# Token block steps of a spectral mixing kernel in eight rotating places, with the set loads spread anew

## The chip, the cores and the metric

The kernel runs on one core of a Trainium2 chip. The metric is the device time of one execution in microseconds (us). The core has five engines that work side by side: TensorE (PE in the profile, with PEld for its weight loads) multiplies matrices into PSUM, VectorE (DVE) does elementwise arithmetic, ScalarE (ACT) does copies and functions, GpSimd (POOL) and SyncE (SP) are used here above all to issue DMA transfers. Semaphores order them.

## The reference

The input is one sequence of S = 2048 tokens with D = 640 channels. It is normalized, goes through a Fourier mixing layer and a gated layer, and both are added to the input:

```python
a = jnp.einsum("bsd,ed->bse", x, dft_hid_re)
b = jnp.einsum("bsd,ed->bse", x, dft_hid_im)
y = jnp.einsum("ts,bse->bte", dft_seq_re, a) - jnp.einsum("ts,bse->bte", dft_seq_im, b)
...
gate = jnp.einsum("bsd,df->bsf", x, W_gate)
up = jnp.einsum("bsd,df->bsf", x, W_up)
gate = gate * (lambda x, dt: x.astype(dt))(gate > 0, gate.dtype)
h = gate * up
return jnp.einsum("bsf,fd->bsd", h, W_down)
...
x = A_x
xn = _layernorm(x, axis=-1)
return x + _A_ref(xn, A_dft_seq_re, A_dft_seq_im, A_dft_hid_re, A_dft_hid_im) + _B_ref(xn, B_W_gate, B_W_up, B_W_down)
```

The gated layer has F = 1728 columns. All data are fp32.

## The kernel before, in words

Every fp32 operand of TensorE is split into a high part (a copy rounded to the fp32r type, made by ScalarE) and a low part (the operand minus its high part, made by VectorE); `split` at L124 and L125 does both. A product of two operands is then three matmuls, high by high, high by low and low by high (`mm3`, L130 to L132). All block products are arranged as in Strassen's method, with seven products of sums and differences of blocks in place of eight.

The program has three phases.

1. **Mixing along the sequence.** The 2048 output positions are worked in four chunks c of 512. For each chunk, the Fourier matrices come from HBM in pieces of 128x1024 (`raw`, six buffers; `tk`, four) and are multiplied by the normalized tokens, which lie in `xs_early` and `xs_late`. A unit such as `T30` is one stream name (T1, T2, B22, T3, T4) and one group of tokens (0 to 3). T1 and B22 units are 18 matmuls, T2, T3 and T4 units 12. Each unit has a `load` (DMA on SP), a `prepare` (VectorE builds the difference at L613, then `split` into a ring of three `cb` buffers), a `run` (TensorE) and a `finish` (sums at L511 to L600, stored by POOL into `pq`). The normalization of the tokens is done during chunk 0, in a 32 KB region `r1` of each partition (`ln_tile`).
2. **Gate and up.** 26 units over the columns of the gate and up weights (`z`, split into `gw`), multiplied by *sets*: sums and differences of blocks of the transposed normalized tokens, kept split in SBUF (`xs_early` for the sets called A, `r1` for those called B). The 64 columns that are left (1728 - 13 x 128) have the *rest weights* (`st`, split into `wr`, L867 to L870), used first in this phase.
3. **Projection** back, with W_down and the hidden Fourier matrices, and the output.

The sets must be made in phase 1. `token_sets` does it for the first half (q = 1) in six *steps*, numbered 0 to 5. A step loads the row statistics (`mr`, L336 or L354) and a block of transposed tokens (`a` or `ab`, L337 or L355) on POOL's queue, normalizes them on VectorE (L340 and L341, or L360 and L361), makes four differences (L367), splits the results in one or two *halves*, and stores high and low part in HBM (L399 and L400 to `halves`, named `set` in the profile). Steps 0 and 1 have one half of 512 columns, steps 2 to 5 two halves of 1024. `load_halves` later brings the finished sets into SBUF (L687): K units load the four B sets, A units the five A sets. An A set lies where tokens lay in `xs_early`, so it waits for the T2 units that read them.

A list `todo` holds units and steps in program order, and `drive(4, 2)` walks through it: at entry i it first calls what was deferred to i, then the load of entry i, the prepare of entry i - 2, the finish of i - 5 and the run of i - 4. The steps of the tokens stand ten entries apart, starting after the last normalization sums of chunk 0. In phase 1 each engine's order comes from a planner that models times and takes the earliest entry that it believes ready; `tc.keep_in_program_order` fixes the first addition of a step, and `tc.issue_after(ins)` puts an instruction behind `ins` on its engine's queue. In phase 2, TensorE, VectorE and ScalarE follow the program's order, while SP and POOL are planned.

`late["dma"]` is the newest load of a Fourier matrix piece. The weights of phase 2 (`Weights`, L764) are already put behind it. `lead_load` (L962 to L965) brings the first operands of phase 3 into two `stage` buffers; `lead_split` splits them at the end of phase 2.

Before the change, a step of phase 1 works in the two buffers of the pool `stage` (both are taken by one step of two halves), and the high part of each half goes to `hi`, a pool with one buffer.

Of the kernel before, what the change touches and what calls it, by code (L numbers as in the profile page):

```python
# [7 lines left out]
F32 = mybir.dt.float32  # L8
F32R = mybir.dt.float32r
# [3 lines left out]
P = 128  # L13
# [3 lines left out]
W2 = 2 * CH  # L17
HC = CH // 2
NCHUNK = S // CH
# [8 lines left out]
NF = F // P  # L28
# [17 lines left out]
NRAW = 10 * P  # L46
# [12 lines left out]
def fnet_reglu_kernel(  # L59
# [15 lines left out]
    nc = tc.nc  # L75
    keep = ctx.enter_context(tc.tile_pool(name="keep", bufs=1))
# [11 lines left out]
    get_r1 = lambda dtype: r1_p.tile([P, len(SETS_B) * 2 * W2], dtype, name="r1")  # L88
# [6 lines left out]
    halves = dram_p.tile([NSET, P, 2, W2], F32, name="set1")  # L95

    firsts = [dram_p.tile([P, 3, CH], F32, name=f"first{c}") for c in range(NCHUNK)]
    pqd = [dram_p.tile([2, P, KD, CH], F32, name=f"pq{c}") for c in range(NCHUNK)]
# [24 lines left out]
    def split(hi, lo, src):  # L123
        nc.scalar.activation(hi, src, AF.Copy)  # L124
        return nc.vector.tensor_tensor(lo, src, hi.bitcast(F32), op=OP.subtract)  # L125
# [23 lines left out]
    def defer(units, f):  # L149

        deferred.setdefault(now[0] + units, []).append(f)
# [4 lines left out]
    ph1 = ExitStack()  # L156
# [2 lines left out]
    tk = ph1.enter_context(tc.tile_pool(name="tk", bufs=NH))  # L159
    sums = ph1.enter_context(tc.tile_pool(name="sums", bufs=1))  # L160
    small = ph1.enter_context(tc.tile_pool(name="small", bufs=2))
    high_p = ph1.enter_context(tc.tile_pool(name="high", bufs=1))
    late_p = ph1.enter_context(tc.tile_pool(name="late", bufs=1, side="right"))
    xs_late = late_p.tile([P, D * S // P], F32R, name="xs_late")

# [19 lines left out]
    late = {}  # L185
# [133 lines left out]
        pin(high(1, 1))  # L319
        late["ln"] = pin(low(1, 1))[-1].ins  # L320

    def token_sets(q, step, stage=stage, unit=None):

        ch = xt[:, q * W2 : (q + 1) * W2].rearrange("(k p) t -> k p t", p=P)
        st_r = rows[:, q * W2 : (q + 1) * W2]
        tt = nc.vector.tensor_tensor
        part = lambda st, i: st[:, i * CH : (i + 1) * CH]
        t = {}

        if step < 2:  # L330
            cs = slice(step * CH, (step + 1) * CH)

            def load():
                t["mr"], t["a"] = stage(), stage()[:, :CH]
                for i in range(2):
                    nc.gpsimd.dma_start(part(t["mr"], i), st_r[i : i + 1, cs].to_broadcast([P, CH]))  # L336
                nc.gpsimd.dma_start(t["a"], ch[4][:, cs])  # L337

            def make():
                tc.keep_in_program_order(tt(t["a"], t["a"], part(t["mr"], 0), op=OP.add))  # L340
                tt(t["a"], t["a"], part(t["mr"], 1), op=OP.mult)  # L341

            made = [([make], "a", lambda v: halves[X4][:, v, cs], lambda ap: ap)]
            keep_whole = lambda: nc.gpsimd.dma_start(sets[X4][:, cs], t["a"])
        else:
            k, hs = (step - 2) // 2, (step - 2) % 2 * HC
            hs = slice(hs, hs + HC)
            cols = lambda ap: ap.rearrange("p (c t) -> p c t", c=2)
            cs = slice(k * CH + hs.start, k * CH + hs.stop)

            def load():
                t["mr"], t["ab"] = stage(), stage()
                for i in range(2):
                    nc.gpsimd.dma_start(cols(part(t["mr"], i)), cols(st_r[i : i + 1])[:, :, hs].to_broadcast([P, 2, HC]))  # L354
                    nc.gpsimd.dma_start(cols(part(t["ab"], i)), cols(ch[k + 2 * i])[:, :, hs])  # L355

            def make():
                mr, ab = t["mr"], t["ab"]
                for i in range(2):
                    tc.keep_in_program_order(tt(part(ab, i), part(ab, i), part(mr, 0), op=OP.add))  # L360
                    tt(part(ab, i), part(ab, i), part(mr, 1), op=OP.mult)  # L361

            def more():

                mr, ab = t["mr"], t["ab"]
                (a0, a1, b0, b1), (t1, t2, t3, t4) = ([st[:, i * HC : (i + 1) * HC] for i in range(4)] for st in (ab, mr))
                sub = lambda o, i0, i1: tt(o, i0, i1, op=OP.subtract)  # L367
                sub(t1, a1, a0)
                sub(t2, b1, t1)
                sub(t3, b1, a1)  # L370
                sub(t4, b0, t2)

            by_set = lambda ap: ap.rearrange("p (i t) -> p i t", i=4)
            made = [([make, more], "ab", lambda v: halves[B11 : B11 + 4, :, v, cs].rearrange("i p t -> p i t"), by_set),
                    ([], "mr", lambda v: halves[T1 : T1 + 4, :, v, cs].rearrange("i p t -> p i t"), by_set)]

            def keep_whole():
                for i, st in ((B11, t["ab"]), (T1, t["mr"])):
                    nc.gpsimd.dma_start(sets[i : i + 4, :, cs].rearrange("i p t -> p i t"), by_set(st))

        if unit:
            unit(load, made[0][0], keep_whole)
            return

        def begin():
            load()
            for i, (make, name, place, view) in enumerate(made):

                def halve(make=make, name=name):
                    for m in make:  # L390
                        m()
                    src = t[name]
                    if "h" not in t:
                        t["h"] = high_p.tile([P, W2], F32R, name="hi")
                    split(t["h"][:, : src.shape[1]], src.bitcast(F32R), src)

                def keep(name=name, place=place, view=view):
                    src = t[name]
                    nc.gpsimd.dma_start(place(0), view(t["h"][:, : src.shape[1]].bitcast(F32)))  # L399
                    nc.gpsimd.dma_start(place(1), view(src))  # L400

                defer(6 + 2 * i, halve)
                defer(7 + 2 * i, keep)

        todo.append((begin, idle, idle, idle))

    def raw():
# [273 lines left out]
    def load_halves(i):  # L681

        def load():
            if "sets_b" not in late:
                late["sets_b"] = {1: get_r1(F32R)}
            t, b = set_place(1, i)
            nc.sync.dma_start(t[:, b : b + 2 * W2].bitcast(F32), halves[i].rearrange("p v t -> p (v t)"))  # L687

        todo.append((load, idle, idle, idle))

# [20 lines left out]
    def phase(c, names):  # L711


        for n in names.split():
            if n == "K":
                load_halves(first_sets.pop(0))
            elif n == "A":
                load_halves(early_sets.pop(0))
            elif n[0] == "W":
                sums_124(int(n[1]))  # L720
            elif n[0] == "V":
                sums_3(int(n[1]))
            elif n[0] == "B" and n[2] == "1":
                first_stream(int(n[3]), n[:3], int(n[4]))
            else:
                stream(c, n[:-1], int(n[-1]))
            if n == "V3":
                free[0] = len(todo) + 2
            if free[0] is not None and len(todo) >= free[0] and steps:
                token_sets(*steps.pop(0))  # L730
                free[0] = len(todo) + SPACE
# [6 lines left out]
    for c in range(1, NCHUNK - 1):  # L738
        phase(c, "T10 T11 T12 T13 T20 B220 T21 B221 T22 T23 B222 B223 T30 T31 T32 T33 T40 T41 T42 T43")
    assert not steps, len(steps)  # L740
    phase(NCHUNK - 1, "T10 T11 T12 T13 T20 K B220 K T21 K B221 K T22 A T23 A B222 B223 T30 A T31 A T32 A T33 T40 T41 T42 T43")
    assert not early_sets and not first_sets
    drive(4, 2)
    ph1.close()
# [9 lines left out]
    NU = 2 * NF  # L754
# [3 lines left out]
    class Weights:  # L758


        def __init__(self, n):
            self.z2 = pool("z").tile([P, 2 * P + NZ], F32, name="z")
            with tc.issue_after(late["dma"]):
                nc.sync.dma_start(self.z2[:, :NRAW], wgu[n % NF])  # L764
            self.n, self.z = n, self.z2[:, 2 * P :]

        def sums(self):
# [20 lines left out]
    weights, held = {}, {}  # L788
# [76 lines left out]

    def rest_weights():
        rest["st"] = st = stage()[:, :D]  # L867
        nc.sync.dma_start(st, wrest)
        rest["w"] = w = pool("wr").tile([P, 2, D], F32R, name="wr")
        split(w[:, 0], w[:, 1], st)  # L870

# [79 lines left out]
    def pair(k0, n):  # L951

        if k0 < KD:
            return hid[0, k0 : k0 + n], hid[1, k0 : k0 + n]
        f = 2 * (k0 - KD)
        w = wd[f * P : (f + 2 * n) * P].rearrange("(k i p) n -> k i p n", i=2, p=P)
        return w[:, 0], w[:, 1]
# [3 lines left out]

    def lead_load():  # L962
        lead["r"], lead["s"] = r, s = stage(), stage()[:, : 2 * 3 * P].rearrange("p (k n) -> p k n", k=2)
        nc.sync.dma_start(r, pqd[2][0][:, :2])
        nc.sync.dma_start(s, pair(0, 2)[0].rearrange("k p n -> p k n")[:, :, : 3 * P])  # L965

    def lead_split():
        t = get_gw[1]().rearrange("p v z -> p (v z)")
# [12 lines left out]
    def place(i):  # L981
        if i % 2 == 0:
            spare[i // 2] = pool("prep").tile([P, Y12 + 2 * P], F32, name="pw")
        return spare[i // 2][:, i % 2 * W2 : (i % 2 + 1) * W2]
# [280 lines left out]
```

## Time and profile before

| | us |
|---|---|
| median of 3 runs | 1048.72 |
| lowest and highest run | 1046.82 and 1049.37 |
| the profiled execution | 1048.9 |
| its span, first to last instruction | 1047.1 |
| TensorE busy | 1028.8 |
| VectorE busy | 802.6 |
| ScalarE busy | 432.9 |
| GpSimd busy | 103.1 |

The mean granted TensorE clock is 0.995 of full speed. A line of the profile names the source line (L613), the engine, the operation, and the tiles as out<-in. In a timeline, the first two numbers are the start and the length in us, and brackets at the end hold how long the engine was idle before the instruction and what released it. In a list of waits, the numbers are the total in us, how often, and the longest. Phase 1 ends near 418 us, phase 2 near 750 us.

### The profile page before, as it was taken

To read this page: it belongs to the slowest core of one execution; us is meant where nothing else is said; L and a number is where in the kernel's file an instruction comes from. 1 tells how busy PE (TensorE), PEld (TensorE's weight loads), DVE (VectorE), ACT (ScalarE), POOL (GpSimd) and SP (SyncE) were. 2 spreads that over 40 slices of the span, in tenths; PEclk is the share of its full clock that TensorE was granted. 3 is DMA by queue.
4 is the path that set the end of the run, shared out by engine and by line. 5 is a ranking of instruction groups with operands and counts; after the bars stand their busy time and mean duration, and the time that the engine had idled before them with its cause. 6 is when DMAs were issued, how large, how long until landed. Compare 5 with 4: busy or idle time off the path is not lost.

```text
span 1047.1 us, 12457 instructions
## 1 busy us (share of the span) xinstructions
PE 1028.8 (98%) x4528; PEld 848.1 (81%) x4528; DVE 802.6 (77%) x1072; ACT 432.9 (41%) x544; POOL 103.1 (10%) x166
## 2 busy tenths in 40 slices
PE   8999999999799999999999999999999999999998
PEld 7888888887587778888888888888888888888886
DVE  7957977977879677687787988877588666786664
ACT  5754443333333333333343544444355423552521
POOL 2000011102212000431110000010000000000000
PEclk9999999999899999999999999999999999999999
DMA  8974754957858895784355666663598736986453
GB/s 306 348 237 165 260 152 149 340 183 266 304 213 271 338 410 214 214 265 155 145 192 171 209 234 215 232 222 131 178 392 286 219 101 215 386 293 228 151 163 120
DMA packets 101469, 242.73 MB, mean 232 GB/s; under 512 B 11553, under 2 KB 50977, under 8 KB 98849
## 3 DMA queue, kind: packets, MB, share of 16 engines
q1 hardware_dynamic: 83664, 171.68, 48.4%
q0 software_dynamic: 17744, 70.26, 18.5%
q8 instruction: 35, 0.57, 0.2%
q14 instruction: 26, 0.20, 0.1%
HBM read 182.12 MB, written 58.74 MB: 230 GB/s over the span
## 4 chain that ended last, share of the span: by engine, by line
PE 85%; issue 6%; DMA 4%; DVE 3%; POOL 1%; ACT 1%; SPq 0%; ACTq 0%; DVEq 0%; POOLq 0%
PE ps L130 28%; PE ps L131 28%; PE ps L132 28%; PE ps L1162 1%; PE ps L501 1%; DMA raw<-in_dft 1%; DMA set<-st 1%; DMA set<-hi 1%; DMA tk<-in_dft 1%; DVE cb L125 1%; DMA rw<-hd 1%; ACT cb L124 1%; DVE tk L613 0%; PE ps L473 0%; DVE raw L613 0%
## 5 line engine op out<-in xcount | busy, mean ns | idle before, releaser
L132 PE MATMUL ps<-cb,wt 128*128 128x512 f32 x390 | 151.9, 390 | 0.4 <-DVE wt L125 0.4
L130 PE MATMUL ps<-cb,wt 128*128 128x512 f32 x390 | 151.8, 389 | 0.0
L131 PE MATMUL ps<-cb,wt 128*128 128x512 f32 x390 | 151.7, 389 | 0.0
L125 DVE TENSOR_TENSOR cb<-rw,cb 128x1024 fp32r<-128x1024 f32 x83 | 94.1, 1133 | 69.7 <-ACT cb L124 67.8
L124 ACT ACTIVATE cb<-rw 128x1024 fp32r<-128x1024 f32 x83 | 81.9, 987 | 149.4 <-PE ps L132 122.8
L124 ACT ACTIVATE cb<-raw 128x1024 fp32r<-128x1024 f32 x78 | 82.5, 1059 | 125.5 <-PE ps L132 108.0
L125 DVE TENSOR_TENSOR cb<-raw,cb 128x1024 fp32r<-128x1024 f32 x78 | 95.2, 1220 | 39.3 <-ACT cb L124 36.0
L131 PE MATMUL ps<-cb,xs_late 128*128 128x512 f32 x256 | 100.7, 394 | 3.8 <-DVE cb L125 3.8
L130 PE MATMUL ps<-cb,xs_late 128*128 128x512 f32 x256 | 100.2, 393 | 4.4 <-ACT cb L124 4.4
L132 PE MATMUL ps<-xs_early,gw 128*128 128x512 f32 x260 | 101.1, 389 | 0.0
L130 PE MATMUL ps<-xs_early,gw 128*128 128x512 f32 x260 | 101.1, 389 | 0.0
L131 PE MATMUL ps<-xs_early,gw 128*128 128x512 f32 x260 | 101.1, 389 | 0.0
L132 PE MATMUL ps<-cb,xs_late 128*128 128x512 f32 x256 | 100.4, 392 | 0.0
L131 PE MATMUL ps<-cb,xs_early 128*128 128x512 f32 x238 | 92.7, 390 | 1.8 <-DVE cb L125 1.8
L130 PE MATMUL ps<-cb,xs_early 128*128 128x512 f32 x238 | 93.2, 393 | 0.8 <-ACT cb L124 0.8
L132 PE MATMUL ps<-cb,xs_early 128*128 128x512 f32 x238 | 92.1, 389 | 0.0
L121 ACT ACTIVATE gw<-z 128x1024 fp32r<-128x1024 f32 (+1 forms) x52 | 57.6, 1110 | 77.8 <-DVE z L774 75.4
L132 PEld LDWEIGHTS ps<-cb,wt 128*128 128x128 f32 x390 | 73.2, 188 | 15.9 <-DVE wt L125 0.7
L131 PEld LDWEIGHTS ps<-cb,wt 128*128 128x128 f32 x390 | 73.2, 188 | 15.5 <-DVE cb L125 0.2
L130 PEld LDWEIGHTS ps<-cb,wt 128*128 128x128 f32 x390 | 73.2, 188 | 15.2
L121 ACT ACTIVATE u<-ps 128x512 f32<-128x512 f32 x52 | 31.2, 599 | 93.2 <-PE ps L132 93.2
L784 DVE TENSOR_TENSOR gw<-z,gw 128x1024 fp32r<-128x1024 f32 (+1 forms) x52 | 64.7, 1284 | 3.8 <-ACT gw L121 3.8
(192 smaller groups left out, 1937.9 us busy)
## 6 DMA issues: line engine op xcount, KB each, us to landing
raw<-in_dft SPq DMA_DIRECT2D x94, 512.0 KB, 5.7
wt<-wparts SPq DMA_DIRECT2D x66, 256.0 KB, 3.2
z<-in_wgu SPq DMA_DIRECT2D x26, 640.0 KB, 4.0
hd<-ob POOLq DMA_DIRECT2D x26, 512.0 KB, 3.7
rw<-hd SPq DMA_DIRECT2D x24, 512.0 KB, 6.4
wparts<-pw POOLq DMA_DIRECT2D x11, 1024.0 KB, 4.1
tk<-in_dft SPq DMA_DIRECT2D x16, 512.0 KB, 6.6
rw<-pq SPq DMA_DIRECT2D x16, 512.0 KB, 7.3
```

Of the source, the lines that this page charges most:

```text
L121: return nc.scalar.activation(o, i, AF.Copy)
L124: nc.scalar.activation(hi, src, AF.Copy)
L125: return nc.vector.tensor_tensor(lo, src, hi.bitcast(F32), op=OP.subtract)
L130: nc.tensor.matmul(ps, wh, mh, start=first, stop=False, skip_group_check=more)
L131: nc.tensor.matmul(ps, wh, ml, start=False, stop=False, skip_group_check=more)
L132: nc.tensor.matmul(ps, wl, mh, start=False, stop=last, skip_group_check=more)
L501: nc.tensor.matmul(E[c, key], xn_part(j, d)[v == 1], b[c][0][:, int(v == 2), j], start=j == 0 and v == 0, stop=False)
L784: tt(self.w[:, 1, cs], self.z[:, cs], self.w[:, 0, cs].bitcast(F32), op=OP.subtract)
L1162: nc.tensor.matmul(B[key], wr[:, v, es], hr[:, cs], start=False, stop=v == 1, skip_group_check=not new)
```

## The change

A step of phase 1 takes each of its buffers (statistics, block, and one high part for each half) from eight places of 4 KB in turn, in one tile over the 32 KB of `r1`, which the normalization has left by then and which the B sets take afterwards. The pool `high` goes. The two halves of a step are deferred by 6 and 7 entries (before: 6 and 8), and the stores by 8 and 9 (before: 7 and 9). In the last chunk, three of the four K entries and two A entries stand together behind T23, and the fourth K stands at the very end; before, the four K stood between T20 and T22. Every K and A load, the rest weights' load and the lead loads get an instruction behind which they must be issued: the newest matrix load for the first three kinds, the last load of phase 2's weights for the lead. Steps of phase 2 (`unit` and `place` given) work as before.

```diff
@@ -159,7 +159,6 @@
-    high_p = ph1.enter_context(tc.tile_pool(name="high", bufs=1))
@@ -319,7 +318,15 @@
-    def token_sets(q, step, stage=stage, unit=None):
+    def token_sets(q, step, place=None, unit=None):
+
+        def work():
+            if "work" not in late:
+                late["work"] = get_r1(F32)
+            i = late["places"] = (late.get("places", -1) + 1) % 8
+            return late["work"][:, i * W2 : (i + 1) * W2]
+
+        stage = place or work
@@ -390,17 +397,15 @@
                     src = t[name]
-                    if "h" not in t:
-                        t["h"] = high_p.tile([P, W2], F32R, name="hi")
-                    split(t["h"][:, : src.shape[1]], src.bitcast(F32R), src)
+                    t["h" + name] = h = work()[:, : src.shape[1]]
+                    split(h.bitcast(F32R), src.bitcast(F32R), src)
 
                 def keep(name=name, place=place, view=view):
-                    src = t[name]
-                    nc.gpsimd.dma_start(place(0), view(t["h"][:, : src.shape[1]].bitcast(F32)))
-                    nc.gpsimd.dma_start(place(1), view(src))
-
-                defer(6 + 2 * i, halve)
-                defer(7 + 2 * i, keep)
+                    for v, part in enumerate((t["h" + name], t[name])):
+                        nc.gpsimd.dma_start(place(v), view(part))
+
+                defer(6 + i, halve)
+                defer(8 + i, keep)
@@ -684,7 +689,8 @@
             t, b = set_place(1, i)
-            nc.sync.dma_start(t[:, b : b + 2 * W2].bitcast(F32), halves[i].rearrange("p v t -> p (v t)"))
+            with tc.issue_after(late["dma"]):
+                nc.sync.dma_start(t[:, b : b + 2 * W2].bitcast(F32), halves[i].rearrange("p v t -> p (v t)"))
@@ -738,7 +744,7 @@
-    phase(NCHUNK - 1, "T10 T11 T12 T13 T20 K B220 K T21 K B221 K T22 A T23 A B222 B223 T30 A T31 A T32 A T33 T40 T41 T42 T43")
+    phase(NCHUNK - 1, "T10 T11 T12 T13 T20 B220 T21 B221 T22 T23 K K K A A B222 B223 T30 A T31 A T32 A T33 T40 T41 T42 T43 K")
@@ -761,7 +767,7 @@
             with tc.issue_after(late["dma"]):
-                nc.sync.dma_start(self.z2[:, :NRAW], wgu[n % NF])
+                self.ins = nc.sync.dma_start(self.z2[:, :NRAW], wgu[n % NF]).ins
@@ -865,7 +871,8 @@
-        nc.sync.dma_start(st, wrest)
+        with tc.issue_after(late["dma"]):
+            nc.sync.dma_start(st, wrest)
@@ -961,8 +968,9 @@
-        nc.sync.dma_start(r, pqd[2][0][:, :2])
-        nc.sync.dma_start(s, pair(0, 2)[0].rearrange("k p n -> p k n")[:, :, : 3 * P])
+        with tc.issue_after(weights[NU - 1].ins):
+            nc.sync.dma_start(r, pqd[2][0][:, :2])
+            nc.sync.dma_start(s, pair(0, 2)[0].rearrange("k p n -> p k n")[:, :, : 3 * P])
```

## The prediction

> **What bounds the kernel now.** I read the page first: TensorE (PE) is busy for 1028.8 us, 98% of the span. So the question is only where it stands still or runs slowly. The waits of TensorE, listed by who is waited for, give the sizes; the busy time by stretch gives the place and the granted clock.
>
> ```profile
> span 1047.1 us, 12457 instructions
> PE ps L131 <- DVE cb L125: 5.6, 3, 2.5
> PE ps L130 <- ACT cb L124: 5.2, 2, 4.4
> 26.20:261.10 234.90, 234.90 (x1037) 194.14 (x1035) 183.01 (x240) 107.96 (x139) 23.41 (x38) 1.00 0.68 233
> 261.10:276.25 15.15, 8.26 (x36) 6.42 (x36) 13.79 (x20) 4.14 (x4) 2.30 (x3) 0.98 0.78 290
> 276.25:282.65 6.40, 6.40 (x15) 4.63 (x15) 5.17 (x5) 2.12 (x2) 2.01 (x3) 0.50 0.99 289
> 282.65:392.00 109.35, 105.47 (x463) 86.34 (x462) 86.72 (x91) 38.79 (x40) 13.94 (x20) 1.00 0.83 310
> 392.00:1042.90 650.90, 650.49 (x2866) 537.35 (x2864) 492.65 (x663) 264.20 (x329) 54.07 (x91) 1.00 0.63 214
> ```
>
> The columns are stretch, length, then busy time of PE, weight loads, DVE, ACT, POOL, then clock and DMA. From 26.2 to 261.1 us TensorE never stops, and after 392 it loses 0.41 us before the tail. All else is lost between 261 and 392 us, in five stops, which the timeline of TensorE shows:
>
> ```profile
> 263.62 0.50 PE L131 MATMUL ps<-cb,xs_late 128*128 128x512 f32 x1 [2.51 <-DVE cb L125]
> 276.25 1.22 PE L130 MATMUL ps<-cb,xs_late 128*128 128x512 f32 x2 [4.38 <-ACT cb L124]
> 338.58 0.50 PE L131 MATMUL ps<-cb,xs_late 128*128 128x512 f32 x1 [1.34 <-DVE cb L125]
> 347.83 0.50 PE L130 MATMUL ps<-cb,xs_early 128*128 128x512 f32 x1 [0.79 <-ACT cb L124]
> 368.70 0.50 PE L131 MATMUL ps<-cb,xs_early 128*128 128x512 f32 x1 [1.75 <-DVE cb L125]
> ```
>
> They add to 2.51 + 4.38 + 1.34 + 0.79 + 1.75 = 10.77 us. Behind the longest, the clock stands at 0.50 for 6.40 us, so half of that, 3.20 us, is lost too. That is 13.97 us in all, the most that the change can win if it touches nothing else.
>
> **Stops at 261 and 272 us: step 3 of the token work.** The timelines of POOL, VectorE (DVE) and ScalarE (ACT) there:
>
> ```profile
> 251.71 0.73 POOL L355 DMA_DIRECT2D st<-in_xt  x1
> 259.40 0.69 DVE L360 TENSOR_TENSOR st<-st 128x512 f32<-128x512 f32 x1 [4.27 <-DMA st<-in_xt]
> 265.72 0.77 POOL L399 DMA_DIRECT2D set<-hi  x1 [8.24 <-ACT hi L124]
> 270.39 1.06 ACT L124 ACTIVATE hi<-st 128x1024 fp32r<-128x1024 f32 x1 [4.16 <-DVE sa L511]
> 271.48 1.23 DVE L125 TENSOR_TENSOR st<-st,hi 128x1024 fp32r<-128x1024 f32 x1 [1.36 <-ACT hi L124]
> 273.83 1.22 DVE L613 TENSOR_TENSOR raw<-raw,tk 128x1024 f32<-128x1024 f32 x1
> 275.14 1.06 ACT L124 ACTIVATE cb<-raw 128x1024 fp32r<-128x1024 f32 x1 [3.69 <-DVE raw L613]
> ```
>
> VectorE stands 4.27 us at the step's first addition (L360), because POOL issued its load only at 251.71; both `stage` buffers were still in use by step 2. The low part that TensorE wants queues behind it: stop one. Then ScalarE stands at 270.39 with the second `hi<-st`. The row names `DVE sa`, but the first half's store left only at 265.72, and the row below, of the waits of all engines, shows `hi` waiting for that store: there is one `hi` buffer. VectorE loses another 1.36 us, the subtraction at 273.83 comes late, the high part at 275.14 later, and TensorE stops for 4.38 us.
>
> ```profile
> ACT hi L124 <- DMA set<-hi: 10.4, 3, 4.2
> ```
>
> **Stops at 337, 347 and 367 us: step 5, and the SP queue.**
>
> ```profile
> 333.94 1.06 ACT L124 ACTIVATE hi<-st 128x1024 fp32r<-128x1024 f32 x1 [4.05 <-DMA set<-hi]
> 335.03 1.23 DVE L125 TENSOR_TENSOR st<-st,hi 128x1024 fp32r<-128x1024 f32 x1 [0.71 <-ACT hi L124]
> 324.00:347.00 23.00, 21.66 (x95) 17.32 (x93) 22.29 (x29) 8.55 (x9) 3.41 (x5) 1.00 0.76 248
> SPq L868 <- DMA set<-st: 6.4, 1, 6.4
> 348.89 0.76 POOL L400 DMA_DIRECT2D set<-st  x1 [6.73 <-DVE tk L613]
> 356.59 0.86 SPq L687 DMA_DIRECT2D r<-set  x2
> 357.54 0.41 SPq L617 DMA_DIRECT2D raw<-in_dft  x1
> 366.28 1.23 DVE L613 TENSOR_TENSOR tk<-raw,tk 128x1024 f32<-128x1024 f32 x1 [7.43 <-DMA raw<-in_dft]
> ```
>
> In step 5 the single `hi` holds ScalarE again (4.05 us), VectorE waits 0.71 us of 23.00 and is busy for 22.29. On SP, the rest weights' load (L868) stands 6.4 us for a `stage` buffer with chunk 3's matrices behind it; then the set loads (L687) stand until 356.59 for step 5's last store (348.89), and the next `raw` goes only at 357.54. VectorE waits 7.43 us for it and TensorE 1.75.
>
> **The change part by part.** No matmul, addition, copy or transfer is added or taken away; their lengths stay.
>
> *Eight places for the steps.* A step's load no longer waits for the step before it (places of step 4 are those of step 2, twenty units back), so the 4.27 us go. Each half has its own high place, so ScalarE's waits at `hi` (10.4 us) go, and with them the 1.36 and 0.71 us on VectorE. What becomes late next is VectorE itself. A step still brings it this, from the groups by line between 320 and 347 us:
>
> ```profile
> L125 DVE TENSOR_TENSOR st<-st,hi 128x1024 fp32r<-128x1024 f32 x2 | 2.4, 1221 | 0.7 <-ACT hi L124 0.7
> L367 DVE TENSOR_TENSOR st<-st 128x256 f32<-128x256 f32 x4 | 1.5, 418 | 0.0
> L360 DVE TENSOR_TENSOR st<-st 128x512 f32<-128x512 f32 x2 | 1.4, 684 | 0.0
> L361 DVE TENSOR_TENSOR st<-st 128x512 f32<-128x512 f32 x2 | 1.4, 684 | 0.0
> ```
>
> That is 6.7 us. A T3 or T4 unit is 12 matmuls of 0.2265 us (1037 in 234.90 us, above), so 2.72 us, and wants 2.44 us of VectorE (two operations of 1.22): only 0.28 us a unit is spare. So in these two places I let VectorE bound TensorE. Near step 3, stops of 2.51 + 4.38 = 6.89 us less the idle VectorE time that goes, 4.27 + 1.36 = 5.63, leaves 1.26. Near step 5, 1.34 + 0.79 = 2.13 less 0.71 leaves 1.42. Together 2.68 us stay; between nothing (the planner fills earlier slack) and the whole 9.02 I take this, since VectorE's rows there stand without a gap. Steps 2 and 4 lie beside the longer T2 and B22 units, where TensorE had no stop.
>
> *Second half at +7 instead of +8, stores at +8 and +9.* VectorE's 1.22 us and ScalarE's 1.06 come a unit sooner, ahead of one more low part: 0 to 1.22 us for step 3, and for step 5; I take 0, as the subtraction that TensorE ends up waiting for stands behind both halves either way. POOL's two stores move back; behind them stand only the stores of sums and the next step's load, which now has a whole step to land. If that cover fails the 4.27 us return.
>
> *The set loads (K, A).* Three K go behind T23's matrix, the fourth behind T43's; each is put behind the newest matrix load on SP. The matrices of T21 to T23 pass them, so the 7.43 us wait and the 1.75 us stop go. The K still cannot go before step 5's last store. What queues behind them now is T30 to T33. T30 is 192 matmuls behind chunk 3's first (72 of T1, 48 of T2, 72 of B22), 43.5 us at 0.2265: near 391 us if T10 begins at 347.83, while the K stood until 356.59. With that cover gone a late T30 would stop TensorE one for one; I take 0, with bounds of 0 and the 1.75 us of today's stop. A wait for TensorE's reads of xs_early, as they do today.
>
> *Rest and lead.* The 6.4 us on SP end: T10's loads, now issued from 341.69, move up, worth nothing beyond the 0.79 us already counted. The rest weights now land later. The rows that bound this:
>
> ```profile
> 388.25 6.40 SPq L617 DMA_DIRECT2D raw<-in_dft  x4
> 409.49 0.80 SPq L764 DMA_DIRECT2D z<-in_wgu  x2
> 410.62 0.72 ACT L124 ACTIVATE wr<-st 128x640 fp32r<-128x640 f32 x1
> 417.56 0.39 PE L130 MATMUL ps<-xs_early,wr 128*128 128x512 f32 x1
> 701.80 0.33 SPq L764 DMA_DIRECT2D z<-in_wgu  x1
> 746.72 1.78 ACT L124 ACTIVATE gw<-st 128x1024 fp32r<-128x1024 f32 x2
> ```
>
> The last matrix goes by 394.65 and ScalarE wants `st` at 410.62: 16 us for a load and one K, today's K loads included in 1.75 us of damage at most. Cost 0; at worst, behind both z loads, it leaves at 410.3 and TensorE wants the split at 417.56, so 7 us less a landing. The lead loads go from 378 and 412 us to behind 701.80 and are wanted at 746.72: 45 us of cover, cost 0.
>
> **Sum.** The profiled execution took 1048.9 us (span 1047.1 and 1.8 around it), 0.2 above the median of the runs, 1048.72. So 1048.9 - 10.77 - 3.20 + 2.68 = 1037.6, and 1037.4 against the median.
>
> **The clock.** The 2.51 us stop was followed by matmuls at full clock up to 271.9 (0.98 over that stretch), the 4.38 us stop by 0.50. The Trainium skill, TensorE: Matmul & The Clock Gate, Part 1, says that half clock follows at least one idle window of about 3.4 us, and that this window runs freely. This trace agrees: 4.38 brought it, 2.51 did not; by it the remaining pieces keep full clock unless they join into one stop over 3.4 us.
>
> **Rivals.**
> *One long stop stays.* At the hand-over from chunk 1 to chunk 2 the T43 subtraction stays late, because step 3's halves are now bunched. Against it: the DMA wait behind it goes. Price: 4.38 + 3.20 stay instead of 1.26, 1037.4 + 6.3 = 1043.7. By the page's rule, named above, the same stop costs its clock again.
> *The loads do not come earlier.* The planner keeps a step's load behind the stores of the step before, now at +8 and +9, one unit ahead of the load. For: POOL's row at 251.71. Then 2.51 and 4.38 and the clock stay, the rest goes: 1048.7 - 3.88 + 1.42 = 1046.3; if SP also keeps its order, no change.
> *Slower.* The whole planned order of the first phase shifts, and the bunched 2.44 + 2.12 us on VectorE and ScalarE stop TensorE in steps 2 to 5 long enough for the clock: four stops like the longest, 4 x (4.38 + 3.20) = 30.3, against 13.97 won: 1065. It decides from three such stops (22.7 us): 1057. Against it: steps 2 and 4 lost nothing although they waited for `hi` too.
>
> **How the numbers follow.** Forecast 0.58 (own range 1034.7, all 13.97 won, to 1041), one long stop 0.20, loads not earlier 0.06, no change at all 0.04, slower 0.12. A difference under 0.3%, 3.1 us, cannot be told from none, which puts 1046.3 there too. So faster 0.78, same 0.10, slower 0.12. The range of 1034.0 to 1046.5 takes in the first three and leaves out the last two, 0.16, and a little below.
>
> **What would show it.** Right: no VectorE wait for DMA st<-in_xt, no ScalarE wait for a store, clock 1.00 from 26 us on, T21's matrix issued before the first set load, the rest load behind the last matrix, gap-free at the first `wr` matmul. Wrong: a stop over 3.4 us beside a step's halves, `raw` landing after its subtraction is due in chunk 3, or a wait for `wr`.

## The result, and the profile after

The changed kernel takes 1038.21 us (median of 4 runs, 1037.96 to 1038.98), against 1049.05 us for the kernel before on the same chip: 0.9901 of it, with a 95% interval of 0.9884 to 0.9918. On another chip, further down, the same pair gives 0.9882 (0.9863 to 0.9901). The profiled execution took 1038.98 us, with a span of 1037.0.

The waits of TensorE and the busy time by stretch, after (columns as before):

```profile
PE ps L130 <- ACT cb L124: 1.8, 2, 1.4
PE ps L131 <- DVE cb L125: 1.5, 1, 1.5
26.20:255.00 228.80, 228.80 (x1010) 189.24 (x1010) 181.53 (x240) 105.66 (x136) 26.28 (x42) 1.00 0.68 236
255.00:275.00 20.00, 18.18 (x73) 14.28 (x72) 19.62 (x24) 8.16 (x8) 1.53 (x2) 0.91 0.95 353
275.00:316.00 41.00, 41.00 (x183) 33.94 (x182) 33.02 (x36) 15.76 (x16) 8.54 (x12) 1.00 0.74 258
316.00:340.00 24.00, 22.51 (x99) 18.00 (x98) 24.00 (x30) 9.91 (x10) 4.67 (x7) 1.00 0.80 298
```

The two waits were 5.2 and 5.6 us before. The stop at chunk 3's T20 is gone. Around step 3 (255 to 275 us) TensorE still loses 1.82 us and around step 5 (316 to 340) 1.49. In the second of these stretches VectorE is busy for 24.00 us of 24.00, in the first for 19.62 of 20.00: TensorE now waits for an engine that works almost without a pause. The stops in the timeline of TensorE, after:

```profile
269.60 0.73 PE L130 MATMUL ps<-cb,xs_late 128*128 128x512 f32 x2 [1.42 <-ACT cb L124]
270.74 1.22 PE L130 MATMUL ps<-cb,xs_early 128*128 128x512 f32 x2 [0.40 <-ACT cb L124]
331.39 0.50 PE L131 MATMUL ps<-cb,xs_late 128*128 128x512 f32 x1 [1.49 <-DVE cb L125]
```

And VectorE ahead of the first one, the same place where it waited for DMA st<-in_xt and for ACT hi before. No brackets, so no idle time: the low parts of step 3 (`r<-r`), two pairs of sums, the T43 difference (L618) in a row.

```profile
262.49 2.35 DVE L125 TENSOR_TENSOR r<-r 128x1024 fp32r<-128x1024 f32 x2
264.76 1.28 DVE L516 TENSOR_TENSOR sa<-ps,sa 128x512 f32<-128x512 f32 x2
265.96 1.28 DVE L519 SCALAR_TENSOR_TENSOR sb<-sb,sa 128x512 f32<-128x512 f32 x2
267.16 1.22 DVE L618 TENSOR_TENSOR raw<-raw,tk 128x1024 f32<-128x1024 f32 x1
```

The span fell by 10.1 us. The stops account for 10.77 - 3.31 = 7.46, the clock for 3.20 - 1.71 = 1.49 (half clock for 3.42 us after, below). Another 0.86 us lie ahead of step 3: without any stop of TensorE from 26.2 us on, unit B223 begins at 244.91 us instead of 245.77. I do not count them for the change: two traces of the changed kernel differ by 0.47 us there (VectorE's first addition of step 0 is at 165.74 and 166.21, before at 166.60). And the 0.37 us wait at the start of phase 3 is 0.19. Together 10.0.

### The profile page after: what moved, and what is told of

Same layout as the page of the kernel before. It is cut to its first block, busy times and chain, and to the rows that moved or that the text cites. A ratio compares the mean times of both kernels' runs of the same rounds, so it can differ in the third digit from the quotient of the medians.

```text
span 1037.0 us, 12454 instructions
## 1 busy us (share of the span) xinstructions
PE 1026.3 (99%) x4528; PEld 846.5 (82%) x4528; DVE 802.5 (77%) x1072; ACT 433.4 (42%) x544; POOL 102.8 (10%) x166
## 4 chain that ended last, share of the span: by engine, by line
PE 93%; DVE 4%; DMA 1%; ACT 0%; issue 0%; SPq 0%; ACTq 0%; DVEq 0%
PE ps L132 30%; PE ps L131 30%; PE ps L130 30%; DVE cb L125 1%; PE ps L506 1%; PE ps L1170 1%; DMA rw<-hd 1%; DVE raw L618 1%; DVE r L125 0%; ACT cb L124 0%; PE ps L478 0%; DMA r<-in_x 0%; DVE r L374 0%; DVE r L367 0%; DVE r L368 0%
## 5 line engine op out<-in xcount | busy, mean ns | idle before, releaser
L130 PE MATMUL ps<-cb,wt 128*128 128x512 f32 x390 | 151.8, 389 | 0.0
L130 PE MATMUL ps<-xs_early,gw 128*128 128x512 f32 x260 | 101.2, 389 | 0.0
L130 PE MATMUL ps<-cb,xs_late 128*128 128x512 f32 x256 | 99.3, 391 | 1.4 <-ACT cb L124 1.4
L130 PE MATMUL ps<-cb,xs_early 128*128 128x512 f32 x238 | 92.8, 393 | 0.4 <-ACT cb L124 0.4
L130 PEld LDWEIGHTS ps<-cb,wt 128*128 128x128 f32 x390 | 73.2, 188 | 15.2
```

What stands on the lines that cost most here:

```text
L130: nc.tensor.matmul(ps, wh, mh, start=first, stop=False, skip_group_check=more)
```

## The experiments

Ratios are to the kernel before in the same job, since that kernel took between 1049.05 and 1051.68 us in the four jobs.

**The places alone, and the loads alone.** The first takes the old kernel with the new `token_sets` and nothing else of the diff; the second the changed kernel with the old `token_sets` and its `high` pool.

```diff
 # e1_places, against the kernel before
-    high_p = ph1.enter_context(tc.tile_pool(name="high", bufs=1))
-    def token_sets(q, step, stage=stage, unit=None):
+    def token_sets(q, step, place=None, unit=None):
...
 # e2_loads, against the changed kernel: the same lines put back
```

> The kernel before with the eight places and the new deferral alone; set loads, rest and lead loads as before. By the theory of the prediction each cause has its own stop: the step stops shrink to about 1.3 and 1.4 us with no long one, the 1.75 us stop in chunk 3 (VectorE waiting for a raw load behind the set loads) stays. That is the changed kernel plus 1.75, about 1040.0 us. Rival: the place stops were hidden behind the SP stops and the two only pay together; then this stays above 1044 us.

> The changed kernel with the token steps put back (two stage buffers, one hi buffer, old deferral); set loads, rest and lead loads as changed. Theory: only the 1.75 us stop of chunk 3 goes, perhaps 0.8 us of the stop before it; the stops of 2.5 and 4.4 us at step 3 and the half clock behind them stay: 1046.5 to 1047.3 us against 1049.05 before. Rival: the rest load that held SP for 6.4 us was what made the stops around step 5; then those go too and the time is near 1045 us.

Measured: places alone 0.9923 (0.9904 to 0.9942), 1041.66 us where I expected about 1040.0; loads alone 0.9978 (0.9964 to 0.9992), 1048.01 us. Gains of 0.77% and 0.22% add to the 0.99% of both, so in the main each part has its own stops. TensorE with the places alone, in chunk 3:

```profile
366.77 0.50 PE L131 MATMUL ps<-cb,xs_early 128*128 128x512 f32 x1 [0.82 <-DVE cb L125]
```

The step stops are those of the changed kernel (1.41, 0.40 and 1.50); the stop behind the set loads stays, but at 0.82 us instead of 1.75. VectorE waits 5.29 us there for the raw matrix, where it waited 7.43 us before. This trace also has a stop of 0.82 us at the start of phase 3 (L130 behind the high part of `wt`) that neither before nor after has; what set it was not settled. With the loads alone, stops of 3.10 and 4.08 us at step 3 and 1.35 and 0.79 at step 5 stay and the 1.75 is gone, as forecast. So the rest load's 6.4 us on SP was not the cause of the stops around step 5.

**One high buffer.** The changed kernel with the old `hi` pool for the high parts, and the old deferral with it:

```diff
-                    t["h" + name] = h = work()[:, : src.shape[1]]
-                    split(h.bitcast(F32R), src.bitcast(F32R), src)
+                    if "h" not in t:
+                        t["h"] = high_p.tile([P, W2], F32R, name="hi")
+                    split(t["h"][:, : src.shape[1]], src.bitcast(F32R), src)
...
-                defer(6 + i, halve)
-                defer(8 + i, keep)
+                defer(6 + 2 * i, halve)
+                defer(7 + 2 * i, keep)
```

> The changed kernel, but the high parts of both halves go through one buffer again, with the old deferral (6 and 8, 7 and 9); loads of the steps stay in places. Theory: ScalarE waits for the store of the first half again, about 4 us in steps 3 and 5, VectorE loses 1.36 and 0.71 us by it, and the stops grow by about that: 1040 to 1042 us, with a clock drop at step 3. Rival: with the loads early the wait of ScalarE is hidden by the two units that lie ready, and the time stays at 1038 us.

Measured: 0.9942 (0.9921 to 0.9962), 1043.64 us, above the 1040 to 1042 that I expected. The timelines of ScalarE and TensorE at step 3:

```profile
268.10 1.06 ACT L124 ACTIVATE hi<-r 128x1024 fp32r<-128x1024 f32 x1 [6.37 <-DMA set<-hi]
272.85 1.06 ACT L124 ACTIVATE cb<-raw 128x1024 fp32r<-128x1024 f32 x1 [3.69 <-DVE raw L620]
273.95 1.22 PE L130 MATMUL ps<-cb,xs_late 128*128 128x512 f32 x2 [5.23 <-ACT cb L124]
```

The wait for the store is back, at 6.37 us, and the stop at step 3 grows to 5.23 us, more than the 4.38 of before. Early loads without a second high buffer only let the step arrive sooner at the same wait. By the ratios the second high buffer, with the deferral, is worth 0.41% (0.9942 to 0.9901), and the places for the loads 0.36% (0.9978 with the loads alone to 0.9942); the intervals do not tell these two apart.

**Second half at +8 again.**

```diff
-                defer(6 + i, halve)
+                defer(6 + 2 * i, halve)
```

> The changed kernel with the second half deferred by 8 again and its stores at 9, places and loads as changed. The prediction put the move of the second half at nothing: same time within 0.5 us, stops of about 1.8 and 1.5 us. Rival (the bunched halves are what is left): the stops shrink and the time falls by 1 us or more; or, spread halves were better for one step only and one stop shrinks by up to 1.2 us.

Measured: 0.9899 (0.9879 to 0.9920), the changed kernel's 0.9901; stops of 1.41, 0.41 and 1.50. The move is worth nothing. The planned order of ScalarE and POOL is the same line for line with either number: the planner puts the halves where their inputs are ready.

**More and less VectorE work.** Two kernels have one and two more additions of 128x1024 in step 3, whose result nobody reads:

```diff
                 sub(t4, b0, t2)
+                if step == 3 and not unit:
+                    e = extra_p.tile([P, W2], F32, name="ex")
+                    for _ in range(1):
+                        tt(e, ab, mr, op=OP.add)
```

> The changed kernel with one more VectorE addition of 128x1024 (1.22 us, its result is not read) in step 3. Theory: the stop at step 3 grows by 1.1 to 1.2 us one for one, to about 3.0 us, and half clock follows it in every run: the changed kernel plus 1.2 to 2.9 us. Rival: slack elsewhere takes it, no growth.

> The same with two more additions (2.44 us). Theory: the stop at step 3 grows to about 4.1 us, with 3.4 to 6.8 us of half clock behind it (1.7 to 3.4 us lost): the changed kernel plus 2.3 to 5 us, near the stop that the kernel before had there. Rival: as above.

And two have less, without the four differences or with narrow ones of 16 columns in place of 256 (both leave out part of what the B sets need):

```diff
 # e4_no_differences
-            made = [([make, more], "ab",
+            made = [([make, more] if unit else [make], "ab",
 # e10_narrow
-                sub = lambda o, i0, i1: tt(o, i0, i1, op=OP.subtract)
+                n = HC if unit else 16
+                sub = lambda o, i0, i1: tt(o[:, :n], i0[:, :n], i1[:, :n], op=OP.subtract)
```

> The changed kernel without the four differences of L374 in the steps of phase 1 (the B sets of the first half then hold other values): 1.4 us of VectorE less in each of steps 2 to 5, nothing moved. Theory (VectorE bounds TensorE beside T3 and T4): the stops of 1.82 us at step 3 and 1.49 us at step 5 shrink by about 1.4 us each, to about 0.4 and 0.1, the half clock behind the first goes: about 1035 us. Rival (the stops are the planner's order or a late load): they stay at 1.8 and 1.5 and the time at 1038.

> The changed kernel with the four differences of a step in phase 1 cut from 256 columns to 16 (the B sets of the first half then hold other values in the columns left out); order and waits stay as they are. That takes about 1 us of VectorE from each of steps 2 to 5. Theory (VectorE bounds TensorE there): the stops of 1.82 us and 1.49 us shrink by about 1 us each, to 0.8 and 0.5, and no half clock follows: 2 to 4 us under the changed kernel. Rival: the planned order alone makes the stops; they stay.

Measured: one more 0.9902 (0.9876 to 0.9929), two more 0.9921 (0.9892 to 0.9950), narrow 0.9858 (0.9840 to 0.9876), where the changed kernel in the narrow one's job has 0.9882. TensorE at step 3 with one more, with two more, and with narrow differences:

```profile
270.35 0.73 PE L130 MATMUL ps<-cb,xs_late 128*128 128x512 f32 x2 [1.95 <-ACT cb L124]
272.08 0.80 PE L130 MATMUL ps<-cb,xs_early 128*128 128x512 f32 x1 [1.00 <-ACT cb L124]
```

```profile
271.62 1.15 PE L130 MATMUL ps<-cb,xs_late 128*128 128x512 f32 x2 [3.08 <-ACT cb L124]
273.36 0.80 PE L130 MATMUL ps<-cb,xs_early 128*128 128x512 f32 x1 [0.59 <-ACT cb L124]
```

```profile
268.64 0.73 PE L130 MATMUL ps<-cb,xs_late 128*128 128x512 f32 x2 [0.41 <-ACT cb L124]
269.78 0.50 PE L130 MATMUL ps<-cb,xs_early 128*128 128x512 f32 x1 [0.40 <-ACT cb L124]
```

The two stops add to 0.81 us with about 1 us less (each of the step's four differences takes 0.17 us instead of 0.42), 1.82 as changed, 2.95 with 1.22 us more, 3.67 with 2.44 more, where I expected 4.1. Up to one addition they follow VectorE's work nearly one for one. The second adds only 0.72, and the rows show why: the first stop grows by 1.13, from 1.95 to 3.08, but the two matmuls behind it now run at half clock and take 1.15 us instead of 0.73, which hides 0.41 of the second stop. At step 5 the narrow differences leave a stop of 0.56 us instead of 1.49. The whole times of the kernels with one more and with narrow differences do not differ from the changed one's beyond the intervals, so there the stops carry the reading. With one more, half clock did not follow in every run, as I had expected, since one of its four runs has a mean clock of 0.999.

Leaving the differences out went the other way: 1.005 (1.0029 to 1.0070), slower than before, and my expectation missed. ScalarE:

```profile
291.70 1.06 ACT L124 ACTIVATE r<-r 128x1024 fp32r<-128x1024 f32 x1 [13.88 <-DMA r<-rows]
```

The differences overwrite the statistics, and without them nothing held back the copy of that buffer until VectorE was done; the planner put it ahead of ScalarE's other work, and ScalarE stood 13.88 us for the load. TensorE then stopped for 7.48 us. That kernel changed an order besides a duration, so it says nothing about VectorE; the narrow differences keep the dependence.

**The steps beside the long units.** If VectorE is the bound beside T3 and T4 (0.28 us to spare in a unit), the steps should lie beside T1 and B22.

```diff
-    SPACE = 9
+    SPACE = [9, 4, 6, 14, 6, 9]
...
-                free[0] = len(todo) + SPACE
+                free[0] = len(todo) + SPACE.pop(0)
 # e9_long_units_b
+    SPACE = [9, 5, 6, 15, 5, 9]
```

> The changed kernel with the steps placed anew in the list: steps 2 to 5 begin at entries 61, 68, 83 and 90 (before 66, 76, 86, 96), so that their halves fall beside T1, T2 and B22 units and none beside T3 or T4. Theory (VectorE has only 0.28 us a unit to spare beside T3 and T4, and this is all that is left of the stops): the stops of 1.82 us at step 3 and 1.49 us at step 5 go, with the half clock of up to 1.7 us behind the first, and the time falls to 1033.5 to 1035 us. Rival (the planner's order at the hand-over of chunks makes the stops, or a step costs TensorE its stop wherever it lies): stops of 1 us and more turn up beside the steps' new places and the time stays within 1 us of 1038.2.

Measured: 0.9855 (0.9831 to 0.9878), 1033.93 us. Both stops are gone; two of 0.52 and 0.53 us are left beside chunk 2's first units, the first of them behind a raw load. A last job put the changed kernel, this one and a variant on one chip:

> The changed kernel once more, on the chip of the next three, so that these can be compared with it: 0.990 of the kernel before.

> The steps beside the long units once more: 0.985 to 0.986 of the kernel before, 4 to 5 us under the changed kernel on the same chip.

> As the kernel with the steps beside the long units, with begins at 62, 69, 85 and 91: the halves of step 4 come two to three entries later than there, where stops of 0.52 us were left beside T10 to T20 of chunk 2. Theory: these two stops go, 1 us less, 1033 us or 0.984 to 0.985 of the kernel before. Rival: the halves of steps 4 and 5 are now five or six entries apart, VectorE is loaded again and stops of 1 us come beside B222; no gain over it.

Measured: 1039.05 us (0.9882, 0.9863 to 0.9901) for the changed kernel, 1035.22 (0.9849, 0.9831 to 0.9866) and 1034.19 (0.9840, 0.9818 to 0.9862) for the two others. The variant beats the kernel before and the changed one. Its time does not tell it apart from the other spacing, and its trace hardly does: the repeat of the other spacing has one stop of 0.51 us left, the variant none. Its waits of TensorE, all that are listed, and its busy time from 26.2 us on:

```profile
PE ps L506 <- DVE xs_early L231: 1.4, 2, 0.9
PE ps L112 <- DVE warm L108: 1.0, 1, 1.0
PE ps L506 <- ACT xs_early L230: 0.3, 1, 0.3
26.20:400.00 373.80, 373.80 (x1651) 309.50 (x1650) 305.81 (x373) 161.34 (x191) 43.24 (x67) 1.00 0.74 265
400.00:1025.00 625.00, 625.00 (x2755) 516.63 (x2754) 473.92 (x641) 256.28 (x321) 52.37 (x88) 1.00 0.63 216
```

Nothing of phase 1 is left between TensorE's matmuls after the start. VectorE's work has not shrunk (305.81 us busy up to 400 us, 303.92 in the changed kernel); it only lies beside other units.

**The clock.** Half clock followed in every trace whose step 3 had a stop of 1.8 us or more. Half clock lasts 3.41 us or a multiple of it: twice that in before, for example, and three times that once without the differences. Counting from its start in steps of 3.41 us, these stretches hold the time that decided; the first four rows are of after, the next two of before, and the last two are the stretch ahead of half clock with the loads alone and with one more addition. The number behind the length is TensorE's busy time, with its matmuls in parentheses; the third from the right is the clock:

```profile
267.31:270.72 3.41, 1.61 (x6) 0.68 (x5) 3.41 (x4) 2.12 (x2) 0.76 (x1) 1.00 0.65 191
270.72:274.14 3.42, 3.40 (x8) 2.71 (x9) 3.34 (x3) 1.06 (x1) 0.00 (x0) 0.50 1.00 346
328.70:332.11 3.41, 1.92 (x9) 1.18 (x8) 3.41 (x4) 2.53 (x3) 0.75 (x1) 1.00 1.01 401
332.11:335.52 3.41, 3.41 (x17) 2.81 (x16) 3.41 (x6) 0.00 (x0) 0.00 (x0) 1.00 1.01 414
```

```profile
262.12:265.54 3.42, 1.92 (x8) 1.61 (x9) 3.42 (x7) 1.33 (x2) 0.00 (x0) 1.00 0.95 349
265.54:268.95 3.41, 3.41 (x16) 2.74 (x15) 3.41 (x5) 0.68 (x1) 0.77 (x1) 1.00 0.83 281
```

```profile
259.80:263.21 3.41, 0.82 (x4) 0.36 (x2) 3.41 (x5) 0.00 (x0) 0.00 (x0) 1.00 1.03 404
```

```profile
267.92:271.33 3.41, 1.21 (x5) 0.35 (x3) 3.41 (x5) 1.42 (x2) 0.76 (x1) 1.00 0.72 226
```

A stretch with 1.61, 1.21 or 0.82 us busy was followed by half clock; one with 1.92 was not, twice. The busy time does not give the limit, though: half clock also followed this stretch of the kernel without the differences, with 2.13 us busy.

```profile
769.91:773.32 3.41, 2.13 (x7) 1.02 (x6) 2.38 (x3) 3.01 (x4) 0.00 (x0) 1.00 1.05 397
```

A matmul that stands alone counts as more than one in a row: the row at 331.39 us, above, has one with 0.50 us, the row at 269.60 two with 0.73. So a stretch broken by stops looks busier than it is. Counted by the matmuls that fall at least partly into it, the stretches do separate: of all stretches at full clock that hold matmuls of 128x512 alone, in the traces of all kernels here, those with 7 or fewer were followed by half clock, and those with 8 or more were not.

## Why the prediction was right or wrong

- **The time.** Forecast 1037.4, measured 1038.21, within its own range. Against the profiled executions, 1037.6 and 1038.98. That it came out so near is in part luck: the stops were 0.63 us more than forecast and the clock cost 1.71 that the sum did not have, while the earlier start (0.86) and the shorter wait at phase 3 (0.18), which no term forecast either, took 1.04 back.
- **What stays when the waits go.** The step that took VectorE for the next bound held; its size near step 3 was short. Near step 5 it gave 1.42 us and the trace shows 1.49; near step 3 1.26 and the trace shows 1.42 + 0.40 = 1.82. Together 3.31 where the sum had 2.68. Most of the difference is the 0.40: in the trace of before the two matmuls behind the long stop ran at half clock, 1.22 us instead of 0.73, which is long enough to hide the second wait. The runs with more and less VectorE work show that the first of the two stops is VectorE's work, and the moved steps that it is the place of it; the 0.40 stayed with the narrow differences too.
- **The clock, put at nothing.** This term failed, and with it the sign that named clock 1.00 from 26 us on: half clock for 3.42 us, 1.71 us lost in the profiled execution. I had read the trace of before as the Trainium skill has it (TensorE: Matmul & The Clock Gate, Part 1: at least one idle window of about 3.4 us), and concluded that pieces under 3.4 us keep full clock. The rows above differ from that: 1.80 us of idle time in a stretch of 3.41 was enough, and the 2.51 us stop of before, which cost no clock, fell in two stretches, 1.00 us in one and 1.50 in the next. The measurement decides. The agreement that the prediction claimed rested on two stops.
- **Loads a whole step early.** Right, by more than forecast. POOL issues the block of each of steps 2 to 5 in two pieces (L362), eight in this phase. The third and fourth are step 3's, at 195.43 and 196.64 us, ahead even of the stores of step 2; before, step 3's went at 251.71 and 252.44. VectorE's first addition of step 3 (L367) is at 254.19 and did not wait, so the 4.27 us went:

```profile
195.43 0.72 POOL L362 DMA_DIRECT2D r<-in_xt  x1 [9.41 <-DVE r L347]
196.64 0.74 POOL L362 DMA_DIRECT2D r<-in_xt  x1 [0.49 <-DVE r L348]
248.46 0.73 POOL L362 DMA_DIRECT2D r<-in_xt  x1 [3.44 <-DMA set<-r]
254.19 0.69 DVE L367 TENSOR_TENSOR r<-r 128x512 f32<-128x512 f32 x1
285.35 0.69 DVE L367 TENSOR_TENSOR r<-r 128x512 f32<-128x512 f32 x1
```

  The third row is already step 4's. Its load waits 3.44 us for a store of step 2, whose places step 4 takes and whose last store POOL issued at 243.56. VectorE needs it at 285.35, so the wait costs nothing.
- **The second half at +7.** Put at 0 between 0 and 1.22 us; measured no difference.
- **Set loads.** The 1.75 us went, as the loads alone show, and between 336 and 372 us VectorE waits for no `raw` matrix any more. With the places alone only 0.82 of it stayed, so the two parts share some of it.
- **Rest and lead.** Put at 0. The rest load went at 385.24, its copy ran at 400.68, the first `wr` matmul at 407.63 without a stop:

```profile
385.24 0.42 SPq L875 DMA_DIRECT2D st<-in_wrest  x1
400.68 0.72 ACT L124 ACTIVATE wr<-st 128x640 fp32r<-128x640 f32 x1
407.63 0.39 PE L130 MATMUL ps<-xs_early,wr 128*128 128x512 f32 x1
```

- **Rivals.** One long stop did not stay; it does with one high buffer (5.23 us). The loads of step 3 did come earlier, by 56 us, and the changed kernel's new order brought no stop at a new place.

## What to carry to other kernels

When a wait goes, ask which engine stands in that stretch without a pause, and subtract only its idle time from the stop: that left 2.7 us here, and 3.3 were measured. Then move work of that engine beside units that leave it room; here that gave another 4.9 us on top of the change's 12.2 in the same job. An experiment that leaves work out can also drop a dependence and change the planned order, so shrink the work instead.

## What the runs showed of the hardware that was not expected

In the steps of phase 1 a stop much shorter than 3.41 us was enough for the clock. It fell to 0.50 for 3.41 us or a multiple of it, after a stretch of 3.41 us that held 7 matmuls of 128x512 or fewer, and stayed at 1.00 after stretches with 8 or more. A stop of 2.51 us that fell across two stretches cost no clock; 1.80 us of two stops inside one stretch cost 1.71 us. Where the stretches fall differs from trace to trace: in after one begins at 267.31 us, in the second trace of the changed kernel at 268.40, 1.09 later, though the stop there ends only 0.44 later (269.60 and 270.04).

The mean clock of the four runs of the changed kernel was 0.996, 0.999, 1.000 and 0.998. A mean of 1.000 leaves no room for a stretch at half clock, so that run lost no clock at step 3. Which of the others did is not shown, since the profiled one has half clock ahead of 26.2 us as well (0.93 there).
